# A gated mix of a state-space layer and a long convolution: mirrored lower halves, products over all frequencies at once, additions by accumulating transfers, loads spread by chunks

## The chip, the cores and the metric

The kernel runs on one core of one Trainium2 chip. The metric is the device time of one execution in microseconds. Three runs of the kernel before gave 442.48, 444.34 and 444.47 us; the median is 444.34. The engines are named as in the profile: PE is TensorE (PEld its weight loads), DVE VectorE, ACT ScalarE, POOL GpSimd, SP SyncE.

## The reference

Inputs are bf16, with S = 2048 rows and D = 1024 columns. The result is `g * a + (1 - g) * b`.

```python
x = A_x
g = sigmoid((x * gate_w).sum(-1, keepdims=True))
# a: a diagonal complex state space of P = 1024 states
Lam_bar = exp(dt * Lam); B_bar = ((Lam_bar - 1) / Lam)[:, None] * Bmat
Bu = einsum("bld,pd->blp", x, B_bar)
for t in range(L): h = Lam_bar * h + Bu[:, t]
a = 2 * einsum("blp,dp->bld", hseq, Cmat).real + x * Dskip
# b: a 4-tap shift of k, times v, then a causal convolution over all 2048 rows
kv = shift(k, shift_k) * v
y = irfft(rfft(kv, 2 * S) * rfft(ssm_k, 2 * S))[:S].astype(bf16)
b = x * (y + kv * ssm_D)
```

## The kernel before

The work has two stages. The first is the convolution, over eight chunks of 128 of the 1024 columns. The second is the state space, over four blocks of 512 rows (`tb`), each with four groups `g` of 256 states.

A chunk of the convolution goes like this. Time is cut in four blocks of 512. `taps` multiplies the transposed k (`kT`, columns on the partitions) by diagonal matrices `dg` of the four taps, and `times_v` multiplies the result by the transposed v, the lower half of each block read backwards. The transform of a block of 512 is made with tables of 256 rows, so the block is folded first: `fold_K` forms upper half plus and minus mirrored lower half of the convolution kernel with the matrices `ident` and `refl`, `fold_V` does the same for v times k with `PM`. Both are matmuls whose results ScalarE brings from PSUM to `eok` and `eov`. `fwd_K` and `fwd_V` then make the spectra `Kh` and `Vh` of 512 frequencies in four tiles (`psk`, `psv`, 128 frequencies each). `products` multiplies the spectra of the four blocks as complex numbers, each kernel block with each earlier or equal block of v, and sums them in `G`; it works on two halves of two frequency tiles each, in bf16 on VectorE (operations `t<-Kh,Vh` and `G<-G,t`). `inverse` goes back to time (`psz`), ScalarE moves the result to `cv`, and SP writes it to the scratch tensor `cv_scr` in DRAM.

The state space: `Bu` multiplies x by B (`bu`), ScalarE moves the result to `U`; `scan` turns it by the tables `TCi`, `TSi`, runs the recurrence as four scans (`W`), turns back by `TC`, `TS` and leaves `hb`; `Cy` multiplies by C (`psy`). `turn_table` makes the four tables of 128 states on ScalarE and VectorE, one per convolution chunk. The rest (`scale_b`, `scale_a`, `finish`) mixes the row tiles with the gate and writes them out; two of its additions are accumulating transfers issued by POOL (`gather`), and `loads` reads `cv_scr` and x again.

Every instruction of an engine is put in the order in which the program states it, by the helper `put` (line 97 of the profile, so nearly all groups carry that line). The order is written out by hand: generators such as `products`, `inverse` or `turn_table` are advanced a step at a time (`step`, `run`) in the loop over chunks (lines 764 to 819), so chunk c's products, chunk c-1's inverse, chunk c+1's spectra and chunk c+2's taps run side by side. In one turn of that loop TensorE's order is foldk, psz (half), psk (half), foldv, psz (half), psv (half), taps, psk (half), psv (half). After the loop (lines 829 to 861) the last chunk's products and inverse run beside the first `Bu`. SP issues all transposing loads, plain loads and stores in program order: per chunk `kT`, `kn`, `vT`, one table of B (`load_BT`, two transposes) or of x (`load_xT`), and the `cv_scr` stores; the C tables (`load_CT`) come in parts from line 832 on.

Memory is given out by pools with a number of buffers: 3 for loads (`ld`), 6 for spectra (`kvh`), 4 for `G`, three pairs of PSUM banks and two single banks.

Of the kernel before, what the change touches and what calls it, by code (L numbers as in the profile page):

```python
# [20 lines left out]
def kernel(  # L21
# [38 lines left out]
    TB = 512  # L60
# [3 lines left out]
    NFI = 4  # L64

# [5 lines left out]
    cv_scr = dram.tile([S, D], BF16, name="cv_scr")  # L71
# [3 lines left out]
    wk = pool("wk", 3)  # L75
# [4 lines left out]
    def w4(shape, dt, name):  # L80
        return wk.tile(shape, dt, name=name, tag="w4")
# [6 lines left out]

    def ps1(tag):
        return psum1.tile([128, 512], F32, name=tag, tag=tag)  # L90
# [49 lines left out]
    kv_pool = h3pool(h3, "kvh", 6)  # L140
    g_pool = h3pool(h3, "gh", 4)
    cv_pool = h3pool(h3, "cv", 2)
    tab_pool = h3pool(h3, "tab", 1)
    ld = h3pool(h3r, "ld", 3, side="right")
    ks_pool = h3pool(h3r, "ks", 2, side="right")
    eo_pool = h3pool(h3r, "eo", 2, side="right")
# [5 lines left out]
    prow = rows_[64:96, 0:128]  # L152

    nc.scalar.dma_start(out=skr, in_=B_shift_k.rearrange("(j p) k -> j p k", p=128))
    for i, ap in enumerate((A_Lambda_re, A_Lambda_im, A_log_dt, gate_w)):
        nc.scalar.dma_start(out=prow[i * 8:(i + 1) * 8, :], in_=ap.rearrange("(j p) -> j p", p=128))
# [4 lines left out]
    def load(which, c):  # L161
        cc = slice(c * 128, (c + 1) * 128)
        if which == "kn":

            t = ld.tile([128, NT, 128], BF16, name="kn", tag="ld")
            load_t(t, B_ssm_k[cc, :])
        else:
            t = ld.tile([128, S], BF16, name=which, tag="ld")
            load_t(t, (kf if which == "kT" else vf)[:, cc])
        lds[which, c] = t  # L170

    load("kT", 0)
    load("vT", 0)
# [5 lines left out]
    def load_BT(g):  # L179
        for c, src in enumerate((A_B_re, A_B_im)):  # L180
            load_t(BT[g][:, c], src[g * 256:(g + 1) * 256, :])

    def load_xT(tb, home=None):
        xT = (home or xt_pool).tile([128, ND, TB], BF16, name="xT")
        load_t(xT, xf[tb * TB:(tb + 1) * TB, :])
        xTs[tb] = xT
# [35 lines left out]

    zeros = w4([128, 512], BF16, "zeros")
    put("dve", V.memset, zeros, 0.0)
    pih = consts.tile([128, 1], F32, name="pih")
    put("dve", V.memset, pih, math.pi / 2.0)
# [8 lines left out]
    colm_i = iota_i32([128, 2], [[256, 2]], 1, 2, "colm")  # L235
    fr_i = iota_i32([128, 2, 256], [[2, 2], [4, 256]], 1, 0, "fr_")
# [6 lines left out]
    pcol = consts.tile([128, 4 + KS, ND], F32, name="pcol")  # L243
    gwb = consts.tile([128, ND], BF16, name="gwb")
    psp = ps1("p1")[:, 0:32 + ND * KS]
    raise_clock(3)
    for k in range(KS):
        mm(psp[:, 32 + ND * k:32 + ND * (k + 1)], skr[:, :, k], ident[32:32 + ND, 32:32 + ND], True, True)
    raise_clock(6)
    copy(pcol[:, 4:], psp[:, 32:].rearrange("p (i j) -> p i j", j=ND))  # L250

    def dgs(c, on_dve=False):
        dg = ks_pool.tile([128, KS, 128], BF16, name="dg", bufs=1)
        for k in range(KS):
            if on_dve:
                ts(dg[:, k], ident, pcol[:, 4 + k, c:c + 1], None, ALU.mult)
            else:
                act(dg[:, k], ident, func=ACT.Identity, scale=pcol[:, 4 + k, c:c + 1])
        return dg

    dg0 = dgs(0, True)
    colm = consts.tile([128, 2], F32, name="colm")
    ts(colm, colm_i, 1.0 / 4096.0, None, ALU.mult)
    fr_ = u4([128, 512], F32, "fr_")
    copy(fr_, flat(fr_i))
    hf = u4([128, 2, 512], F32, "h")
    for mt in range(2):
        ts(hf[:, mt], fr_, colm[:, mt:mt + 1], None, ALU.mult)
    rqf = reduced(flat(hf), 1024)
    put("dve", V.scalar_tensor_tensor, out=flat(hf), in0=rqf, scalar=-1.0, in1=rqf, op0=ALU.mult, op1=ALU.max)  # L270
    PM = consts.tile([128, 2, 2, 128], BF16, name="PM")
    for a in range(2):
        for b in range(2):
            ts(PM[:, a, b], ident, -1.0 if a and b else 1.0, None, ALU.mult)

# [9 lines left out]
    def inverse_angles(h2):  # L285
        hi = (w4 if h2 else u4)([128, 2, 512], F32, "h")
# [3 lines left out]
        rq = (u4 if h2 else w4)([128, 1024], F32, "rq")  # L290
        ts(rq, flat(hi), MAGIC, -MAGIC, ALU.add, ALU.add)
        tt(flat(hi), flat(hi), rq, ALU.subtract)
        return flat(hi)

    def inverse_table(h2, rq):
        sincos(rq, 1024, flat(SI[:, 2 * h2:2 * h2 + 2]), flat(CI[:, 2 * h2:2 * h2 + 2]), -TWO_PI)


    Lre, Lim, logdt = pcol[:, 0], pcol[:, 1], pcol[:, 2]
# [4 lines left out]
    TC = rot_pool.tile([128, NP, TB], BF16, name="TC")  # L304
    TS = rot_pool.tile([128, NP, TB], BF16, name="TS")
    TCi = rot_pool.tile([128, NP, TB], BF16, name="TCi")
    TSi = rot_pool.tile([128, NP, TB], BF16, name="TSi")
# [3 lines left out]

    def state_params():

        mm(psp[:, 0:32], prow, ident[64:96, 64:96], True, True)
# [85 lines left out]
    def rev(ap):  # L400

        return ap.rearrange("p (b t) -> p b t", t=512)[:, :, 255::-1]
# [560 lines left out]
```

## Time and profile before

| What | Value |
|---|---|
| median of three runs | 444.34 us |
| the profiled execution | 444.19 us |
| its span, first to last instruction | 442.4 us |
| granted TensorE clock, mean | 0.994 |
| products of chunk 0, 1, 2, 3 begin at | 21.7, 50.2, 74.6, 99.6 us |
| products of chunk 4, 5, 6, 7 begin at | 124.6, 149.6, 174.6, 199.5 us |
| first operation of the first scan begins at | 226.2 us |
| last scan's last operation ends, about | 425.5 us |
| last matmul ends, about | 436.8 us |

The profiled execution took 1.8 us more than its span. The page's first part gives each engine's busy time and its share of the span. The groups give, for operations of one line, engine and shape, how often they ran, their busy time, the mean length of one in ns, and how long the engine stood idle before them and for what. The chain of waits follows the work back from the last instruction: each piece is what the next one waited for. A matmul's length is longer than the distance to the next one, because matmuls are pipelined; distances are read from the chain or from the order of time.

### The profile page before, as it was taken

How to read it: one execution, taken by the hardware profiler on the slowest of the kernel's cores; microseconds unless marked ns; L12 is line 12 of the kernel's file. 1: busy time of each engine (PE TensorE's matmuls, PEld its weight loads, DVE VectorE, ACT ScalarE, POOL GpSimd, SP SyncE). 2: the span in 40 equal slices, each digit the busy share in tenths (PEclk: the TensorE clock that was granted, in tenths of full speed). 3: DMA queues.
4: the chain of work that ended last, by engine and by line, in shares of the span. 5: the costliest groups of instructions: out<-in, count | busy, mean ns of one | idle time of the engine just before them, and what ended most of it. 6: DMA issues, size and time to landing. Idle time of an engine off the chain costs nothing.

```text
span 442.4 us, 5684 instructions
## 1 busy us (share of the span) xinstructions
PE 423.1 (96%) x2104; PEld 199.4 (45%) x2142; DVE 421.9 (95%) x662; ACT 260.3 (59%) x320; POOL 27.1 (6%) x41
## 2 busy tenths in 40 slices
PE   8888899999999999979999999999999999999994
PEld 3434354544545454534444544444444444444442
DVE  7897999999999999999999999999999999999973
ACT  3796978979797979695552423443324432567102
POOL 2000000000000000000000000011011100223100
PEclk9998999999999999999999999999999999999999
DMA  7685294756558291135608941144474546297512
GB/s 144 144 134 105 49 184 100 140 111 149 125 102 184 60 205 24 25 68 100 115 12 159 176 135 24 25 119 111 99 172 96 147 139 166 38 207 162 118 45 98
DMA packets 128062, 49.94 MB, mean 113 GB/s; under 512 B 118169, under 2 KB 118177, under 8 KB 128034
## 3 DMA queue, kind: packets, MB, share of 16 engines
q1 hardware_dynamic: 123920, 42.22, 43.3%
q0 software_dynamic: 4032, 7.34, 9.6%
q8 instruction: 16, 0.26, 0.2%
q14 instruction: 12, 0.10, 0.1%
q10 hardware_dynamic: 82, 0.02, 0.0%
HBM read 8.67 MB, written 8.39 MB: 39 GB/s over the span
## 4 chain that ended last, share of the span: by engine, by line
PE 75%; DVE 12%; ACT 8%; issue 4%; DVEq 0%
PE bu L97 25%; PE psy L97 22%; PE psz L97 9%; PE psk L97 8%; DVE G L97 5%; DVE t L97 4%; PE taps L97 2%; PE foldk L97 2%; PE psv L97 2%; ACT Vh L97 2%; PE p L97 2%; PE foldv L97 2%; ACT eok L97 1%; ACT eov L97 1%; ACT Kh L97 1%
## 5 line engine op out<-in xcount | busy, mean ns | idle before, releaser
L97 PE MATMUL bu<-xT,BT 128*128 128x512 bf16 x499 | 111.6, 379 | 0.6
L97 DVE TENSOR_TENSOR t<-Kh,Vh 128x2048 bf16<-128x2048 bf16 (+3 forms) x128 | 102.3, 820 | 4.1 <-ACT SI L97 2.7
L97 PE MATMUL psy<-CT,hb 128*128 128x512 bf16 x470 | 105.2, 379 | 0.6
L97 PEld LDWEIGHTS <-BT 128*128 128x128 bf16 x512 | 50.0, 98 | 60.2
L97 PEld LDWEIGHTS <-hb 128*128 128x128 bf16 x512 | 49.9, 98 | 59.9
L97 DVE TENSOR_TENSOR G<-G,t 128x1536 bf16<-128x1536 bf16 (+2 forms) x144 | 69.4, 510 | 0.5
L97 ACT ACTIVATE U<-bu 128x1024 bf16<-128x1024 f32 x32 | 32.6, 1022 | 47.1 <-PE bu L97 42.3
L97 DVE TENSOR_TENSOR_SCAN W<-rv,init,A 128x512 bf16<-128x512 f32 x48 | 57.8, 1266 | 0.0
L97 PE MATMUL psz<-G,CI 128*128 128x512 bf16 x128 | 48.6, 379 | 2.0 <-DVE G L97 2.0
L97 PE MATMUL psz<-G,SI 128*128 128x512 bf16 x128 | 48.5, 379 | 0.0
L97 ACT ACTIVATE Kh<-psk 128x1024 bf16<-128x1024 f32 x32 | 32.6, 1028 | 10.7 <-PE psk L97 10.0
L97 ACT ACTIVATE ga<-psy,gcols 128x1024 bf16<-128x1024 f32 x8 | 8.9, 1114 | 46.3 <-PE psy L97 46.3
L97 PE MATMUL taps<-kT,dg 128*128 128x512 bf16 (+3 forms) x128 | 30.8, 385 | 1.6 <-ACT Vh L97 1.5
L97 ACT ACTIVATE Vh<-psv 128x1024 bf16<-128x1024 f32 x32 | 30.9, 1024 | 0.9 <-PE psv L97 0.9
L97 POOL DMA_DIRECT2D pbb<-gd x12 | 10.5, 871 | 342.4 <-ACT gd L97 330.3
L97 PE MATMUL psk<-eok,CF 128*128 128x512 bf16 (+1 forms) x96 | 26.5, 366 | 3.9 <-ACT eok L97 2.1
L97 ACT ACTIVATE cv<-psz 128x1024 bf16<-128x1024 f32 x16 | 16.4, 1027 | 23.0 <-PE psz L97 23.0
L97 PEld LDWEIGHTS <-CF 128*128 128x128 bf16 x160 | 15.7, 98 | 22.2 <-issue 7.0
L97 PE MATMUL psk<-eok,SF 128*128 128x512 bf16 (+1 forms) x89 | 24.7, 373 | 0.4
L97 ACT ACTIVATE BT<-psy,gcols 128x1024 bf16<-128x1024 f32 x6 | 6.7, 1111 | 30.6 <-PE psy L97 30.6
L97 PEld LDWEIGHTS <-SF 128*128 128x128 bf16 x160 | 15.9, 99 | 18.2 <-issue 3.5
L97 PE MATMUL psv<-eov,CF 128*128 128x512 bf16 x64 | 19.3, 379 | 3.0 <-ACT eov L97 2.2
(139 smaller groups left out, 570.0 us busy)
## 6 DMA issues: line engine op xcount, KB each, us to landing
cv_scr<-cv SPq DMA_DIRECT2D x32, 128.0 KB, 2.1
pbb<-cv_scr SPq DMA_DIRECT2D x12, 256.0 KB, 2.7
xr<-in_A_x_dram SPq DMA_DIRECT2D x12, 256.0 KB, 4.2
pbb<-gd POOLq DMA_DIRECT2D x12, 256.0 KB, 3.3
ga<-xr POOLq DMA_DIRECT2D x8, 256.0 KB, 3.3
out_dram<-ga SPq DMA_DIRECT2D x8, 256.0 KB, 2.0
out_dram<-BT SPq DMA_DIRECT2D x8, 256.0 KB, 2.0
BT<-cv_scr SPq DMA_DIRECT2D x4, 256.0 KB, 3.3
```

Of the source, the lines that this page charges most:

```text
L97: i = f(*a, **kw)
```

## The change

It touches nearly all of the first stage, and the joint to the second.

- v is loaded untransposed by plain copies (`v`, rows on the partitions), from chunk 2 on in pairs of chunks. `tap_sums` therefore makes its result with rows on the partitions: `kT` is the stationary operand, 128 rows at a time, and `dg` the moving one, 64 matmuls of 128 columns for a chunk. `kT` has 16 zero columns ahead, set by POOL.
- The folding matmuls are replaced. `mirror_K` and `mirror` only mirror the lower half with `refl` (into `lo`, by ScalarE); the difference is made by VectorE (`eok[:, 0]`, `ev`), the sum by an accumulating transfer (`eok[:, 1]`, `ks`). Chunks 0 to 2 keep `fold_K`; chunks 1 and 7 make the sum of v by VectorE, chunk 0 works from PSUM.
- From chunk 1 on `products` runs once over all 512 frequencies. It keeps the second factor's products in `T2` (memory of `BT[2]`) and subtracts and adds them at the end; the products with the next kernel block are added into `G` by an accumulating transfer of 128 x 3072, which VectorE does itself in the second half of chunk 0 and in chunk 7. The spectra `Kh` of even chunks lie in `BT[3]`.
- TensorE's order in a turn is psz (half), mirror, psz (half), psk of all four tiles, mirror_K, taps, psv of all four tiles.
- `turn_table` rounds with one operation on VectorE instead of two; its last two additions become one accumulating transfer into `TCSi`. The state's small factors (`c2r`, `c2i`, `mc2i`) are made with fewer, wider VectorE operations.
- In the start, `dg` of chunk 0 is made by ScalarE, `PM` is gone, `kT` of chunk 0 comes in two halves; one half of the inverse tables is made before the loop, one in chunk 0.
- Loads: B tables 0 and 1 in chunks 2 and 4, x blocks 0 and 1 in halves in chunks 5 and 6, B tables 2 and 3 in the last chunk, all C tables after the convolution's memory is given back.
- In the last chunk `Bu(0, 0)` stands ahead of the inverse of chunk 6 on TensorE.
- `cv_scr` is laid out by chunk, so its stores are long pieces and its loads short ones. PSUM has four pairs of banks and no single ones. Work memory of the scans lies where the convolution's was.
- At the end each row tile's last eight matmuls are followed by its own finishing work, and the last tile is written in two halves.

```diff
-    psum = pool("psum", 3, space=bass.MemoryType.PSUM)
-    psum1 = pool("psum1", 1, space=bass.MemoryType.PSUM)
+    psum = pool("psum", 4, space=bass.MemoryType.PSUM)
...
-    kv_pool = h3pool(h3, "kvh", 6)
-    g_pool = h3pool(h3, "gh", 4)
+    kv_pool = h3pool(h3, "kvh", 3)
+    g_pool = h3pool(h3, "gh", 2)
...
+            w = 1 if c < 2 else 2
...
+            move(t.rearrange("p n k d -> p n (k d)"),
+                 vf.rearrange("(n p) d -> p n d", p=128)[:, :, c * 128:(c + w) * 128])
...
+        act(rq, trow[0], func=ACT.Identity, scale=thn[:, pi:pi + 1], bias=magic)
         yield
-        ts(rq, h, MAGIC, -MAGIC, ALU.add, ALU.add)
-        tt(rq, h, rq, ALU.subtract)
+        put("dve", nc.vector.scalar_tensor_tensor, out=rq, in0=rq, scalar=-MAGIC, in1=h, op0=ALU.add, op1=ALU.subtract)
...
-        act(TCi[:, pi], TC[:, pi], func=ACT.Identity, scale=c2r[:, pi:pi + 1])
-        act(TSi[:, pi], TS[:, pi], func=ACT.Identity, scale=c2r[:, pi:pi + 1])
-        yield
-        tt(TCi[:, pi], TCi[:, pi], m[:, 0], ALU.add)
-        tt(TSi[:, pi], TSi[:, pi], m[:, 1], ALU.add)
+        act(flat(TCSi[:, pi]), flat(TCS[:, pi]), func=ACT.Identity, scale=c2r[:, pi:pi + 1])
+        gather(flat(TCSi[:, pi]), flat(m))
...
+    def mirror_K(c):
+        kb = lds.pop(("kn", c)).rearrange("p (a f) d -> p f a d", f=4)
+        ps = ps2([128, 2, 4, 128], "mirror")
+        for mt in range(2):
+            mm(ps[:, mt], refl[:, 1], kb[:, 1 - mt], True, mt == 0)
+            if mt == 1:
+                mm(ps[:, mt, 0], refl[0:1, 1], sD[:, c * 128:(c + 1) * 128], False, True)
+        eo = eos["k", c] = eo_pool.tile([128, 2, 2, 4, 128], BF16, name="eok")
+        lo = eo_pool.tile([128, 2, 4, 128], BF16, name="lo", bufs=2)
+        act(lo, ps, func=ACT.Copy)
+        act(eo[:, 1], kb[:, 2:4], func=ACT.Copy)
+        yield
+        tt(eo[:, 0], kb[:, 2:4], lo, ALU.subtract)
+        gather(eo[:, 1], lo)
...
+    def tap_sums(kT, dg, h):
+        ps = ps2([128, 8, 128], "taps")
+        for n in range(8):
+            t0 = (8 * h + n) * 128
+            for i in range(KS):
+                k0 = PAD + t0 - i
+                mm(ps[:, n], kT[:, k0:k0 + 128], dg[:, i], i == 0, i == KS - 1)
+        return ps
...
+    def mirror(c):
+        ps = ps2([128, 2, 4, 128], "mirror")
+        for mt in range(2):
+            mm(ps[:, mt], refl[:, 1], kss[c][:, 1 - mt], True, True)
+        return ps
...
+    def times_v(c):
+        ks, v = kss[c], lds.pop(("v", c))
+        tt(ks, ks, v.rearrange("p (b q) d -> p q b d", q=4), ALU.mult)
+        yield
+        lo = eo_pool.tile([128, 2, 4, 128], BF16, name="lo", bufs=2)
+        act(lo, mirror(c), func=ACT.Copy)
+        yield
+        e = eo_pool.tile([128, 2, 4, 128], BF16, name="ev")
+        tt(e, ks[:, 2:4], lo, ALU.subtract)
+        if c in (1, NC - 1):
+            tt(ks[:, 2:4], ks[:, 2:4], lo, ALU.add)
+        else:
+            gather(ks[:, 2:4], lo)
...
+    def products(c, h=0, home=u4, by_dma=True):
...
+        mult(0, 0, None, G)
+        yield
+        n1 = mult(1, 0, W1)
+        if by_dma:
+            gather(G[:, :, 1:], n1)
+        yield
+        t2 = mult(0, 1, T2)
+        yield
+        n2 = mult(1, 1, W2)
+        if not by_dma:
+            tt(G[:, :, 1:], G[:, :, 1:], n1, ALU.add)
+        n3 = mult(2, 1, home([128, 4 * w], BF16, "t"))
+        tt(t2[:, :, 1:], t2[:, :, 1:], n2, ALU.add)
+        n2 = mult(3, 1, home([128, 2 * w], BF16, "t"))
+        tt(t2[:, :, 2:], t2[:, :, 2:], n3, ALU.add)
+        n1 = mult(2, 0, W2[:, 0:4 * w])
+        n3 = mult(3, 0, W2[:, 4 * w:])
+        tt(t2[:, :, 3:], t2[:, :, 3:], n2, ALU.add)
+        tt(n1[:, :, 1:], n1[:, :, 1:], n3, ALU.add)
+        yield
+        tt(G[:, :, 2:], G[:, :, 2:], n1, ALU.add)
+        yield
+        tt(G[:, 0], G[:, 0], t2[:, 1], ALU.subtract)
+        tt(G[:, 1], G[:, 1], t2[:, 0], ALU.add)
...
+        tabs, back, prod = turn_table(c - 1, u4), inverse(c - 1), products(c)
+        step(old)
+        step(tabs)
+        step(back)
+        step(tv)
+        steps(prod, 3)
+        run(tv)
+        step(old)
+        if nn < NC:
+            dg = dgs(nn)
+        run(back)
+        run(old)
+        if c in (1, 3):
+            load("v", c + 3)
+        elif c == NC - 2:
+            load_xT(1)
+        fwd_K(n)
+        step(prod)
+        fk = none
+        if nn < NC:
+            fk = mirror_K(nn)
+            step(fk)
+            taps(nn, dg)
+        step(tabs)
+        step(prod)
+        run(fk)
+        run(prod)
+        if nn < NC:
+            tv = times_v(nn)
+            step(tv)
+        fwd_V(n)
+        old = tabs
...
+        prod, back = products(c, 0, room, False), inverse(c - 1)
+        load_BT(2, 0)
+        load_BT(2, 1)
+        load_BT(3, 0)
+        load_BT(3, 1)
...
+        Bu(0, 0)
+        steps(prod, 3)
...
-    for pi in range(4, NP):
+    for pi in range(NP):
         load_CT(pi)
+    move(drow, bc(A_Dskip.rearrange("(o d) -> o d", o=1), [128, D]))
...
     for tl in range(4):
-        Cy_g(tb, tl, pss[tl][0], NG - 1, False, [0])
-    for tl in range(4):
-        Cy_g(tb, tl, pss[tl][0], NG - 1, True, [1])
-        if tl % 2 == 0:
+        Cy_g(tb, tl, pss[tl][0], NG - 1, True)
+        if tl == 1:
             scale_a(t0 + tl, pss[tl][1])
-    for tl in (1, 0, 3, 2):
         run(fins[tl])
```

More of the change, by code (lines that the diff above doesn't have):

```diff
@@ L678, in scale_b, with Cy_g @@
         gather(pbb, gd)
[L680 removed]
+    def Cy_g(tb, tl, ps, g, last):
         tsl = slice(tl * 128, (tl + 1) * 128)
[L682 removed]
+        for j in range(2):
             for c in range(2):
```

593 lines of the change are left out of this document (279 added, 314 removed).

## The prediction

> **What bounds the kernel now.** I read the page's first two parts, then the busy time stage by stage with the borders at the chunks, then the chain of waits, then the groups by shape, last the transfers. The page names no single bound: two engines are nearly full.
>
> ```profile
> span 442.4 us, 5684 instructions
> PE 423.1 (96%) x2104; PEld 199.4 (45%) x2142; DVE 421.9 (95%) x662; ACT 260.3 (59%) x320; POOL 27.1 (6%) x41
> ```
>
> The stages separate them. A stage's columns are its length, then busy time of TensorE, its weight loads, VectorE, ScalarE, GpSimd, then clock and DMA share.
>
> ```profile
> 99.60:124.60 25.00, 24.68 (x126) 12.14 (x127) 24.90 (x46) 21.66 (x29) 0.00 (x0) 1.00 0.63 138
> ...
> 199.50:226.20 26.70, 26.54 (x121) 12.09 (x124) 26.26 (x49) 16.30 (x23) 0.00 (x0) 1.00 0.45 87
> 226.20:425.50 199.30, 198.30 (x1019) 92.17 (x1037) 197.39 (x237) 78.30 (x82) 23.41 (x27) 1.00 0.51 117
> 425.50:436.80 11.30, 11.25 (x52) 4.88 (x51) 4.59 (x7) 1.89 (x2) 0.86 (x1) 1.00 0.20 47
> ```
>
> A convolution chunk takes 25.0 us (products start at 74.6, 99.6, 124.6, 149.6, 174.6): VectorE 24.9, TensorE 24.7, ScalarE 21.7. From 199.5 to 436.8 TensorE has no gap: 237.3 us in which only TensorE counts. The chain of waits (start, length, work) shows the handover, the end, and the pace of a row of matmuls:
>
> ```profile
> 62.40 1.75 PE foldv L97 x16
> ...
> 199.13 0.30 DVE G L97
> 199.44 0.04 issue
> 199.48 2.75 PE psz L97 x12
> ...
> 209.14 3.45 PE psz L97 x16
> ...
> 428.48 6.71 issue
> 435.19 0.25 DVE BT L97
> ```
>
> TensorE waited 1.99 us at 199.48 for the products of chunk 6. So: what is saved before 199.5 moves the dense stretch forward whole; what is saved on VectorE inside it is worth nothing (VectorE idles 6.71 us at the end). Prices come from the groups (mean ns of one):
>
> ```profile
> L97 DVE TENSOR_TENSOR t<-Kh,Vh 128x2048 bf16<-128x2048 bf16 x32 | 37.7, 1219 | 1.2 <-ACT Kh L97 1.2
> L97 DVE TENSOR_TENSOR t<-Kh,Vh 128x512 bf16<-128x512 bf16 x32 | 13.5, 421 | 0.0
> L97 ACT ACTIVATE Kh<-psk 128x1024 bf16<-128x1024 f32 x32 | 32.6, 1028 | 10.7 <-PE psk L97 10.0
> L97 POOL DMA_DIRECT2D pbb<-gd x12 | 10.5, 871 | 342.4 <-ACT gd L97 330.3
> ```
>
> Last the transfers, by queue (packets, MB, share of 16 engines) and by issue (KB each, us to landing):
>
> ```profile
> q1 hardware_dynamic: 123920, 42.22, 43.3%
> q0 software_dynamic: 4032, 7.34, 9.6%
> pbb<-gd POOLq DMA_DIRECT2D x12, 256.0 KB, 3.3
> BT<-xr POOLq DMA_DIRECT2D x4, 256.0 KB, 4.7
> ```
>
> **Parts and costs.** *VectorE in a chunk.* 2048 against 512 elements give 798 ns per 1536: 0.52 ns each and 155 ns fixed. Three neighbours (2048, 2048, 1536) take 3.22 us, not 3.39, so each follows 0.085 us before the last one ends: 0.07 us fixed. Before, a chunk has 39,936 elements in 42 such operations and two f32 ones of 512 (0.95 us): 20.75 + 2.94 + 0.95 = 24.6; measured 25.0, a factor 1.016. After, both halves are one: mults of 4096, 3072, 4096, 3072, 2048, 1024, 2048, 1024, adds of 3072, 2048, 1024, 1024, 2048, 2048, 2048, then ev 1024, eok 1024 and the product with v, 2048: 37,888 elements, 18 operations, one f32 of 512 (0.61). 19.7 + 1.26 + 0.61 = 21.55, times 1.016 = **21.9**. The additions that left (3072 into G, 1024 each for ks and eok, 1024 for TCi/TSi) became accumulating transfers.
>
> *TensorE in a chunk.* 512 columns cost 0.2155 us (16 psz in 3.45). psz 6.9, psk 6.05, psv 3.46 stay. foldk (10, 2.15 us) becomes mirror_K (3, 0.55), foldv (16, 1.75) becomes mirror (2, 0.43). taps keep 8192 columns, but as 64 weight-load and matmul pairs of 128 columns instead of 16 of 512. No row shows such a pair: below is 24.7 ns (64 gate pairs of 1 column, 1.58 us on the chain), above 109 ns (16 foldv pairs of 256 columns, 1.75 us). From 512 columns at 215.5 and 256 at 109.4 a straight line gives 56; I take it, for both neighbours lie on it: 64 x 56 = 3.6. Sum 17.4 + 3.6 = **21.0**; ends 19.0 and 24.4.
>
> The Trainium skill (TensorE: Matmul & The Clock Gate, Back-to-back issue gap) gives about 81 ns for such a pair in a sustained stream. By it taps would cost 5.2 and TensorE 22.6, 0.7 over VectorE. For 512 columns it gives 131 ns, where this trace has 215, so I hold it for the less likely price.
>
> *ScalarE in a chunk.* Evictions follow one another at 0.92: 14 (cv 2, lo 2, Kh 4, ks 2, Vh 4) = 12.9; eok from SBUF 1.04; dg 1.15; hr twice, abs, two sines, m twice 4.2; TCSi as one of 1024 1.04: 20.3 (16 evictions, 20.7 before). It stays under the others by 1 us, which is its whole cover; if it is short, Vh comes late and VectorE's next first product waits.
>
> *The coupling.* Before, products began on the first half of the frequencies while the second was still made. Now the first product waits for all four Vh, the last work of TensorE and ScalarE in the chunk, and VectorE's whole queue stands behind it. psz of the previous chunk can start when G is ready, 1.1 us before that product; 21.0 of TensorE and 1.0 of the last eviction then end at 20.9 of the 21.9: cover 1.0. I take no stall; bounds 0 and 2 us a chunk (ScalarE's longest wait for psk in the row above, 10.7 over 32 evictions, is a third of a microsecond each).
>
> *Accumulating transfers, POOL.* Per chunk four issues (0.87 us each before; POOL had nothing there) move 768 + 3 x 256 KB. 7.34 MB in 9.6% of 442.4 us is 173 GB/s: 9.1 us of all engines. By the hardware queue (42.22 MB in 43.3%: 220 GB/s) kT, kn, a share of v and cv, 1.84 MB, take 8.3, in chunks 2 and 4 with BT 10.7. 17 to 20 of 21.9 us, against 0.63 of 25. G's is consumed 12 us after its issue, by an addition of VectorE with eok, the last G and the product with v behind it; eok's and TCSi's in the next chunk. Tight is ks: it is issued about 8 us after the chunk's first product begins (behind ev, which reads ks), on the queue behind G's, issued at 4 (two products); psv reads it at about 16.5. At the queue's rate it lands at 4 + 1 (issue) + 4.5 (G) + 1.5 + 1.8 (3.3 us to landing less 1.5 of moving) = 13; at half rate 19. I take 13 to 16, for the other queue's share here was 0.63 and falls: no wait.
>
> *Start.* Half loads of kT and a copy of v instead of a transpose let taps begin earlier; dg (0.74) moves to ScalarE, PM (0.49) and five small operations go, but four operations read PSUM in f32 with 1024 elements (512 cost 681 ns, so 1.13 in sequence, 4.5 for 2.7 before). VectorE begins at 2, has 18.2 of its own and about 0.9 of waits: first product at 21.1 (21.7 before). To the first product of chunk 1: two halves 35,328 elements, 31 operations 20.5; ks 2.3; ev, ks, dg, small ones 3.0; waits 0.6: 26.4 against 28.5. ScalarE, which held this stretch before with both inverse tables (6 us), now has four of their six operations there: 19 evictions 17.5, tables 4, small 0.8 = 22.3, under 26.4. Chunk 1 starts at **47.5**, before 50.2; ends 45 and 50.
>
> *Last chunk.* TensorE now runs Bu(0,0) (6.9) ahead of psz of chunk 6, so the 1.99 us wait goes. Next late is psz of chunk 7, at 27.6 in the dense stretch; its products end at about 26: cover 1.6. BT 2 and 3, loaded only there, are four transposes of about 2.7: in by 14, used at 20.7 and 34.5. CT comes whole after the tables are free: SP starts xT(2) at 36 (35.9 before), 5.1, then 16 CT at 1.34 and 4 to land: 67; first used at 70. Cover 3 us; if gone, that stalls TensorE one to one. drow, pbb and xr queue behind on SP to 64, used by ScalarE after 70. The scan's A and hb now lie on memory of the last Kh, Vh and G, which VectorE and TensorE have left by then: nothing. cv written in long pieces and read in short ones lies beside the scan stage, read a step ahead. The fourth PSUM pair removes waits like the 0.51 us of psv for Kh at 195.56: below 1 us a chunk, put at nothing. The tail: both last row halves go through VectorE after the last matmul, 0.2 + 1.4 and the 3.4 from VectorE's end to the span's end: 5.0, before 5.6.
>
> *Sum.* Chunk 1 at 47.5; four chunks 87.6; G of chunk 5 20.7; then TensorE psz, mirror, psk, psv 17.0; dense stretch 237.3; tail 5.0: span 415.1. The profiled execution took 444.19, 1.8 over its span (median shown 444.34): **417**.
>
> **Rivals.** (1) taps pairs above the line, or ScalarE's handshake, set the chunk. For: idle cover is 1 us. At 109 ns, period 24.4: 4 x 2.5, about 1 in chunk 5 and 3 in the start: 431. Midway, 82 ns, period 22.7: 4 x 0.8 + 1 = 421.
> (2) ks lands late and psv, hence Vh and the next first product, waits; five chunks have this order. If transfers queued with transposes land each 256 KB at 4.7 us (the slowest row): 4 + 4 x 4.7 = 22.7, 6.2 late, 5 x 6.2 = 31: 448, slower. Decides from 5.4 us late ((444.2 - 417) / 5). Against: 4.7 contains the fixed part once per transfer; share was 0.63. At 2 us late: 427.
> The Trainium skill (DMA: Bandwidth & Descriptors, Issuing engines are not separate DMA queues) speaks for this rival: whichever engine issues, the same 16 engines do the work, interleaved.
> (3) The late CT or BT stall TensorE 3 to 8 us: 420 to 425.
> No rival is that VectorE sets the scan stage: it starts the scans at 173 + 26 = 199 and needs 199.3, ending at 398, while TensorE ends at 410.
>
> **How the numbers follow.** Forecast 0.57 (412 to 422); rival 1 0.20 (418 to 431); rival 2 0.15, of which 0.08 slower and 0.03 without change; rival 3 0.06; something unseen 0.02, slower. Range 410 to 432: the low end from a start of 45 (2.5), no 1.016 (1.7) and 0.5 us of PSUM waits gone in each of six chunks; the high end is rival 1's. Over 0.5% (2.2 us, about what a measurement here can tell) faster: 0.57 + 0.20 + 0.04 + 0.06 = 0.87; within 0.03; slower 0.10.
>
> **What would show it.** Products of chunks 2 to 5 starting every 22 us with VectorE full; chunk 1 at 47.5; Bu(0,0) from about 173; no TensorE gap for 237 us. taps' 64 matmuls in 3.6 us. Wrong: psv waiting for a DMA into ks, the first product waiting for Vh over 1 us, psy waiting for CT.

## The result and the profile after

The changed kernel takes 415.38 us in the median, the kernel before, run beside it, 443.55: a ratio of 0.936, with a 95% interval of 0.933 to 0.940. Forecast were 417.0 us in a range of 410 to 432. Some executions ran longer at a lower granted clock, one of the changed kernel's four (426.43 us) and three of four of the kernel below that puts the inverse of chunk 6 first, and the ratios leave them out. The profiled execution took 415.12 us, its span is 413.3.

The page's first part and the busy time by stages, of the changed kernel. The columns of a stage are its borders and length, busy time of TensorE, weight loads, VectorE, ScalarE and GpSimd (instructions in brackets), granted clock, DMA share, GB/s.

```profile
span 413.3 us, 6053 instructions
PE 402.1 (97%) x2340; PEld 201.5 (49%) x2378; DVE 399.5 (97%) x470; ACT 253.3 (61%) x307; POOL 53.0 (13%) x74
```

```profile
69.00:90.60 21.60, 21.20 (x149) 11.77 (x149) 21.60 (x21) 20.00 (x27) 3.89 (x5) 1.00 1.19 190
170.90:197.70 26.80, 26.64 (x123) 12.18 (x125) 26.70 (x24) 22.52 (x31) 2.57 (x3) 1.00 0.69 141
197.70:397.00 199.30, 198.24 (x1018) 92.14 (x1037) 197.76 (x237) 78.27 (x82) 23.22 (x27) 1.00 0.61 128
397.00:409.10 12.10, 12.05 (x56) 5.26 (x54) 5.79 (x8) 1.11 (x1) 0.86 (x1) 1.00 0.30 87
```

A chunk lasts 21.6 us where it lasted 25.0, and VectorE is busy for all of it, in 21 instructions instead of 46. The scan stage has the length it had (199.3 us) and starts 28.5 us earlier. The two engines' shares of the span hardly moved, 96% to 97% and 95% to 97%; they say nothing of what was gained.

The groups by shape (instructions, busy us, mean ns, idle time before them) and the transfers (by queue: packets, MB, share of 16 engines; by issue: KB each, median us to landing), of the changed kernel:

```profile
L91 PE MATMUL psz<-G,SI 128*128 128x512 bf16 x128 | 48.5, 379 | 1.9 <-DVE G L91 1.9
L91 PE MATMUL taps<-dg,kT 128*128 128x128 bf16 x512 | 31.1, 223 | 0.0
L91 DVE TENSOR_TENSOR G<-Kh,Vh 128x4096 bf16<-128x4096 bf16 x4 | 9.1, 2282 | 0.0
L91 POOL DMA_DIRECT2D G<-wkh x7 | 8.5, 1221 | 70.5 <-DVE wkh L91 70.5
```

```profile
q1 hardware_dynamic: 117648, 42.22, 47.3%
q0 software_dynamic: 8528, 17.17, 25.4%
G<-wkh POOLq DMA_DIRECT2D x6, 768.0 KB, 7.1
ks<-lo POOLq DMA_DIRECT2D x5, 256.0 KB, 6.9
```

All idle time of TensorE in the chunks that VectorE causes is 1.9 us in five waits for G. The software queue moves 17.17 MB instead of 7.34. The instructions of one chunk in order of time (start, length), VectorE first, then ScalarE, then GpSimd, where a bracket would give idle time ahead:

```profile
87.16 2.35 DVE L91 TENSOR_TENSOR G<-G,BT 128x2048 bf16<-128x2048 bf16 x2
89.43 1.22 DVE L91 TENSOR_TENSOR ks<-ks,v 128x2048 bf16<-128x2048 bf16 x1
90.57 2.28 DVE L91 TENSOR_TENSOR G<-Kh,Vh 128x4096 bf16<-128x4096 bf16 x1
...
86.55 3.77 ACT L91 ACTIVATE Vh<-psv 128x1024 bf16<-128x1024 f32 x4
...
73.24 1.20 POOL L91 DMA_DIRECT2D G<-wkh  x1 [7.35 <-DVE wkh L91]
76.05 0.89 POOL L91 DMA_DIRECT2D ks<-lo  x1 [1.61 <-DVE ev L91]
```

The coupling is in the first four rows: the last Vh ends at 86.55 + 3.77 = 90.32, the first product of the next chunk starts at 90.57 without a wait. It is held up by VectorE's own queue, but only 0.25 us separate it from waiting for ScalarE. The transfer into ks is issued at 76.05 and lands 7.6 us later, at 83.7 (6.9 is the median of the five); psv takes it at 85.9.

Where the 29.1 us of span went (starts of products and of the dense stretch, end of the last matmul):

| Stretch | before | after | gained |
|---|---|---|---|
| start to the products of chunk 1 | 50.2 | 47.4 | 2.8 |
| four chunks | 99.4 | 86.3 | 13.1 |
| products of chunk 5 to the dense stretch | 49.9 | 37.2 | 12.7 |
| dense stretch to the last matmul | 237.3 | 238.2 | -0.9 |
| tail | 5.6 | 4.2 | 1.4 |

Two rows of this table need a second look. What the first row gains is idle time of VectorE: between the first product of chunk 0 and that of chunk 1 it was busy for 25.45 of 28.5 us before and for 26.06 of 26.8 after. Before, 2.65 us of that idle time were a wait for ScalarE's inverse table `SI`. Part of the gain may belong to the clock: in the profile before, the granted clock of this stretch was 0.94, in the profile after 1.00.

```profile
21.70:50.20 28.50, 23.40 (x108) 10.92 (x108) 25.45 (x57) 23.35 (x33) 0.00 (x0) 0.94 0.59 105
```

The kernel before also has spans of 440.7 us at a mean clock of 0.997 to 0.998, beside the profiled 442.4 at 0.994, so up to 1.7 of the 2.8 us may not come from the change. The dense stretch, the other row, did not become slower by 0.9 us; it holds more work. The kernel before ran four matmuls of the inverse of chunk 6 ahead of its wait at 199.48.

```profile
196.47 0.38 PE L97 MATMUL psz<-G,CI 128*128 128x512 bf16 x1
...
197.12 0.38 PE L97 MATMUL psz<-G,SI 128*128 128x512 bf16 x1
```

In the changed kernel these stand behind Bu(0,0), inside the stretch: four times 0.2155 us are 0.86.

### The profile page after: what moved, and what is told of

Same layout as the page of the kernel before. It is cut to its first block, busy times and chain, and to the rows that moved or that the text cites. A ratio compares the mean times of both kernels' runs of the same rounds, so it can differ in the third digit from the quotient of the medians.

```text
span 413.3 us, 6053 instructions
## 1 busy us (share of the span) xinstructions
PE 402.1 (97%) x2340; PEld 201.5 (49%) x2378; DVE 399.5 (97%) x470; ACT 253.3 (61%) x307; POOL 53.0 (13%) x74
## 3 DMA queue, kind: packets, MB, share of 16 engines
q1 hardware_dynamic: 117648, 42.22, 47.3%
q0 software_dynamic: 8528, 17.17, 25.4%
## 5 line engine op out<-in xcount | busy, mean ns | idle before, releaser
L91 PE MATMUL psy<-CT,hb 128*128 128x512 bf16 x502 | 111.4, 379 | 0.6
L91 ACT ACTIVATE U<-bu 128x1024 bf16<-128x1024 f32 x32 | 32.4, 1021 | 48.1 <-PE bu L91 43.3
L91 PE MATMUL psz<-G,SI 128*128 128x512 bf16 x128 | 48.5, 379 | 1.9 <-DVE G L91 1.9
L91 PE MATMUL psz<-G,CI 128*128 128x512 bf16 x128 | 48.5, 379 | 0.1
L91 PE MATMUL taps<-dg,kT 128*128 128x128 bf16 x512 | 31.1, 223 | 0.0
L91 PEld LDWEIGHTS <-kT 128*128 128x128 bf16 x512 | 29.8, 100 | 0.7
L91 ACT ACTIVATE BT<-psy,gcols 128x1024 bf16<-128x1024 f32 x5 | 5.6, 1113 | 30.4 <-PE psy L91 30.4
L91 PE MATMUL psk<-eok,CF 128*128 128x512 bf16 (+1 forms) x89 | 24.0, 360 | 0.0
L91 DVE TENSOR_TENSOR wkh<-BT,Vh 128x3072 bf16<-128x3072 bf16 (+4 forms) x20 | 21.8, 1109 | 0.0
L91 PEld LDWEIGHTS <-CI 128*128 128x128 bf16 x128 | 12.5, 98 | 18.2 <-issue 3.3
L91 DVE TENSOR_TENSOR wkh<-Kh,Vh 128x3072 bf16<-128x3072 bf16 (+2 forms) x16 | 21.3, 1348 | 0.0
L91 DVE TENSOR_TENSOR hb<-TCS,W 128x2048 bf16<-128x2048 bf16 (+1 forms) x17 | 19.8, 1163 | 1.2
```

The costliest lines, as they stand in the source:

```text
L91: i = f(*a, **kw)
```

## The experiments

The theory: a chunk is as long as the sum of VectorE's own instructions, the loop through TensorE and ScalarE (G of one chunk to the first product of the chunk after the next) lies just under it, and what is saved ahead of the dense stretch moves the end one for one. Rivals: TensorE (21.2 of 21.6 us busy) is the bound already; the transfers pace the chunk.

### VectorE makes the sum into G again

```diff
+        by_dma = False
         if by_dma:
             gather(G[:, :, 1:], n1)
```

> One part undone: the sum of 128 x 3072 into G is made by VectorE in every chunk, where the changed kernel leaves it to an accumulating transfer in all but the second half of chunk 0 and chunk 7. Theory A (a chunk is as long as VectorE's own instructions, 21.6 us of 21.6): such an addition took 1.75 us alone and 1.66 in a row, so the chunk becomes 23.2 to 23.3; chunks 1 to 5 and half an addition in chunk 0 make 5 x 1.66 + 0.85 = +9.2, about 424.6 us. Rival B (transfers or TensorE, with 21.2 of 21.6 busy, pace the chunk as much as VectorE does): taking 768 KB off the queues gives some of it back, and the time rises by 5 us or less.

Measured: 425.33 us, span 423.0, 9.7 more than the changed kernel's. Two stages of one chunk each, and the landing of ks's transfer:

```profile
71.20:94.45 23.25, 22.57 (x151) 12.21 (x151) 23.25 (x21) 18.29 (x25) 2.67 (x4) 0.96 0.59 118
94.45:117.70 23.25, 21.35 (x149) 11.67 (x149) 23.25 (x22) 21.94 (x30) 2.67 (x4) 0.99 0.74 150
```

```profile
ks<-lo POOLq DMA_DIRECT2D x5, 256.0 KB, 3.7
```

The period is 23.25: 1.67 more, the price of the operation, and VectorE is still busy for all of it. Theory A holds; the transfers give nothing back though their share of the chunk falls from about 1 to 0.6 or 0.7. ks lands in 3.7 us instead of 6.9: half of its way is G's transfer ahead of it.

### Two halves again

```diff
-        k = 2 if c == 0 else 1
+        k = 2 if c < NC - 1 else 1
...
+    def both(c):
+        hs = [products(c, h) for h in range(2)]
+        for _ in range(6):
+            for p in hs:
+                step(p)
+            yield
...
-        tabs, back, prod = turn_table(c - 1, u4), inverse(c - 1), products(c)
+        tabs, back, prod = turn_table(c - 1, u4), inverse(c - 1), both(c)
```

> One part undone: products of chunks 1 to 6 are made in two halves of the frequencies again, in turns (each operation on the first half, then on the second). The elements stay; a chunk gets 15 more operations of VectorE at 0.07 us fixed: +1.05, and one issue more on GpSimd (about 1 us). Theory A: period 22.6, over 5 chunks +5.3, about 420.7 us. Rival B (the earlier start of the first product, which needs only two of the four Vh, gives some back, or TensorE gets G earlier): VectorE is full, so nothing is to be had from it, unless its operations then wait less than 0.1 us a chunk; under +3.

Measured: 420.49 us, span 418.8 (+5.5). One chunk:

```profile
70.35:92.94 22.59, 21.49 (x149) 11.71 (x149) 22.59 (x35) 20.96 (x28) 5.15 (x6) 1.00 1.00 184
```

The period is 22.59, 1.02 longer for 15 operations more: 0.068 us of fixed cost for each, where the prediction had read 0.07 from three neighbours. The earlier first product gave nothing back. So the width of the operations is worth 5 us of the 28, the accumulating sum into G nearly 10. These two, and the order in the last chunk further down, are the parts of the change that were undone alone; the smaller sums by transfer, the mirroring matmuls and the start were not.

### TensorE: the mirror of v made twice and four times

```diff
-        for mt in range(2):
+        for mt in range(2) if c < 2 else (0, 1) * 2:
             mm(ps[:, mt], refl[:, 1], kss[c][:, 1 - mt], True, True)
```

(`* 4` in the second kernel.)

> TensorE gets 0.43 us more in each turn from chunk 1 on: the two mirroring matmuls of v are made twice, the second time over the first, with the same result. Theory A with the coupling (the first product waits for the last Vh, which came 0.25 us before it): 0.43 less 0.25 is 0.2 us a chunk for chunks 1 to 5, and 0.43 whole in the turn of chunk 6, where nothing on VectorE stands behind: +1.3, about 416.7; period 21.8. Rival B (TensorE's own free time, 0.5 to 0.7 us a chunk, takes it): period 21.6, only the last turn pays, +0.4. Rival C (TensorE is the bound already): 6 x 0.43 = +2.6.

> The same with three repeats, 1.29 us more of TensorE in a turn. With the coupling's 0.25 us of cover: 5 x 1.04 + 1.29 = +6.5, about 421.9, period 22.6, and the first product now waits for Vh. With a cover of 1.0 us, as predicted: 5 x 0.29 + 1.29 = +2.7, about 418.1, period 21.9. TensorE the bound already: 6 x 1.29 = +7.7.

Measured: ratios to the kernel before of 0.940 (0.938 to 0.943; span 414.4, +1.1) and 0.949 (0.947 to 0.951; 420.71 us, span 418.8, +5.5). VectorE's first products and one stage of the four-fold mirror:

```profile
92.52 2.29 DVE L91 TENSOR_TENSOR G<-Kh,Vh 128x4096 bf16<-128x4096 bf16 x1 [0.75 <-ACT Vh L91]
114.92 2.29 DVE L91 TENSOR_TENSOR G<-BT,Vh 128x4096 bf16<-128x4096 bf16 x1 [0.75 <-ACT Vh L91]
137.34 2.29 DVE L91 TENSOR_TENSOR G<-Kh,Vh 128x4096 bf16<-128x4096 bf16 x1 [0.75 <-ACT Vh L91]
```

```profile
92.50:114.90 22.40, 22.30 (x155) 12.38 (x155) 21.66 (x19) 20.76 (x28) 3.92 (x5) 1.00 0.85 169
```

Now TensorE is full (22.30 of 22.40) and VectorE waits 0.75 us a chunk for Vh, as rival 1 would have it. The period rose by 0.83 for 1.29 added: the cover is 0.46 us, between the 0.25 that one chunk of the trace shows and the predicted 1.0. The sum 5 x 0.83 + 1.29 = 5.4 comes close to the 5.5 measured, but in part by luck: in the rows, the products of chunk 6 start 111.7 us after those of chunk 1 where it was 107.9 (+3.85, for the first of the five periods is 22.1), 0.6 us come from a later start whose code is the same, and 1.0 comes after them. The smaller repeat agrees with such a cover: there it is 108.3 us (+0.09 a chunk for 0.43 added), 0.25 us come from the start, and the last turn pays 0.4. TensorE was not the bound, but it is half a microsecond from it: by this cover, the taps at the 82 ns of the midway case of rival 1 (1.7 us more) would have cost some 1.2 us a chunk, an estimate.

### ScalarE: one eviction more, early or late in the chunk

```diff
             act(cv, ps, func=ACT.Copy)
+            if l2 == 0 and c < NC - 2:
+                act(cv, ps, func=ACT.Copy)
```

```diff
             act(of_tile(VH[c], fi), ps, func=ACT.Copy, scale=2.0 / 1024.0)
+            if fi == 0 and c > 1:
+                act(of_tile(VH[c], fi), ps, func=ACT.Copy, scale=2.0 / 1024.0)
```

> ScalarE gets one eviction more per turn, early in the chunk: the first half of cv is brought from PSUM twice (0.92 us in sequence) for chunks 0 to 5. ScalarE's sum rises from 20.0-20.5 to 20.9-21.4 of 21.6. In the changed kernel ScalarE waited behind this place three to four times in a chunk (0.34 and 0.49 us for psk, 0.47 for taps): theory A, the wait for psk and taps takes the extra work, the last Vh comes as before and the period stays 21.6: 0 to +1 us. Rival B (ScalarE's cover is only the 0.25 us by which the last Vh came before the first product, wherever the work is put): 0.92 less 0.25 makes 0.67 a chunk, +3.4 us.

> The same 0.92 us of ScalarE, but in its last row of the chunk: the first of the four Vh is brought twice, from chunk 2 on. Theory A: four evictions stand in one row from the last ks to the first product, with nothing to take it up but the cover of the coupling; the four-fold mirror left 0.46 us of it unseen (1.29 added, period 21.57 to 22.40). So 0.92 less 0.25 to 0.46 is 0.5 to 0.7 a chunk for chunks 1 to 5, and in the last turn psv of chunk 7 may wait for a PSUM pair: +2.5 to +4.3, 418 to 420 us, period 22.1 to 22.2. If a chunk's cover were the predicted 1.0 us: 0 to +0.5.

Measured: early a ratio of 0.9365 (0.934 to 0.939) and a span of 413.2, that is nothing; late a ratio of 0.953 (0.947 to 0.958), from single executions of 418.5, 420.2 and 423.6 us (a fourth took 424.8), the first of them profiled with a span of 416.7 (+3.4). A stage with the early eviction, and VectorE's first products of chunks 2 to 5 with the late one:

```profile
90.50:112.00 21.50, 21.09 (x149) 11.76 (x149) 21.50 (x20) 21.16 (x29) 3.92 (x5) 1.00 0.83 158
```

```profile
69.16 2.29 DVE L91 TENSOR_TENSOR G<-BT,Vh 128x4096 bf16<-128x4096 bf16 x1 [0.18 <-ACT Vh L91]
91.31 2.29 DVE L91 TENSOR_TENSOR G<-Kh,Vh 128x4096 bf16<-128x4096 bf16 x1 [0.49 <-ACT Vh L91]
113.16 2.29 DVE L91 TENSOR_TENSOR G<-BT,Vh 128x4096 bf16<-128x4096 bf16 x1 [0.18 <-ACT Vh L91]
137.09 2.29 DVE L91 TENSOR_TENSOR G<-Kh,Vh 128x4096 bf16<-128x4096 bf16 x1 [2.27 <-ACT Vh L91]
```

ScalarE at 21.16 of 21.5 us costs nothing as long as the work lies ahead of the waits for psk and taps that take it up; behind them the same 0.92 us makes VectorE wait 0.2 to 0.5 a chunk. That is less than the expected 0.5 to 0.7, so that the +3.4 lies in the expected range by luck: most of it is the 2.27, and that is something else. In that chunk TensorE stood before psv, and the transfer into ks took up to 11.3 us to land:

```profile
131.60 0.59 PE L91 MATMUL psv<-ks,SF 128*128 128x512 bf16 x2 [1.89 <-DMA ks<-lo]
```

The issue was at 120.22, so psv wanted ks 131.60 - 1.89 - 120.22 = 9.5 us after the issue. In the changed kernel's profile psv takes ks 9.2 to 9.8 us after the issue and the landings took 6.6 to 8.8, which leaves covers of 1.0 to 3.2 us in the five chunks; a landing of 11.3 breaks them. The next chunk had such a wait too (1.07 us), and the two-halves kernel had two, the longest 1.3 us. Rival 2's place is real; in the changed kernel's profile it stays just unseen. Whether it also makes the difference between the executions is open, since only one was profiled.

### The transfers delayed

```diff
             gather(G[:, :, 1:], n1)
+            if 0 < c < NC - 1:
+                gather(G[:, :, 1:], n1)
```

> In chunks 1 to 6 the accumulating transfer into G is made twice, so the output counts the products with the next kernel block twice. GpSimd must let the first one land (7 us) before it issues the second, and the issue of ks's transfer stands behind that: about 6 us later than now, and 768 KB more are under way beside it. Rival 2 of the prediction (ks late, psv and the next chunk's first product wait): ks landed at about 83 for a use at 85.4 in the chunk that starts at 69.0, so it comes 3 to 7 us late, and 5 chunks with 0.25 us of further cover make +14 to +32, 430 to 447; the trace shows TensorE's psv waiting for the transfer into ks. If the transfers have room and psv can wait unseen: under +3.

Measured: 449.85 us, 1.7% slower than the kernel before (ratio 1.017, 1.013 to 1.020); the profiled execution is the fastest of the four, with a span of 443.9, +30.6. Waits of TensorE, of VectorE and of GpSimd, in order of time:

```profile
74.72 1.01 PE L91 MATMUL psv<-ks,SF 128*128 128x512 bf16 x2 [10.36 <-DMA ks<-lo]
100.08 0.59 PE L91 MATMUL psv<-ks,SF 128*128 128x512 bf16 x2 [2.74 <-DMA ks<-lo]
...
73.25 1.22 DVE L91 TENSOR_TENSOR G<-G,wkh 128x2048 bf16<-128x2048 bf16 x1 [8.63 <-DMA G<-wkh]
98.30 1.23 DVE L91 TENSOR_TENSOR G<-G,wkh 128x2048 bf16<-128x2048 bf16 x1 [1.17 <-DMA G<-wkh]
...
91.62 1.19 POOL L91 DMA_DIRECT2D G<-wkh  x1 [5.56 <-DMA G<-wkh]
92.36 1.38 POOL L91 DMA_DIRECT2D ks<-lo  x1
```

GpSimd holds ks's issue until the first transfer into G has landed (5.56 us at 91.62). The issue of ks comes 4.7 to 5.5 us later in the chunk than in the changed kernel. Over five chunks psv waited 26.2 us for ks, and VectorE's addition of G waited as well; Vh and the next chunk's products come late behind both. The two longest waits, 10.4 and 6.9 us, are those in which the landing was longer too (14.4 and 11.7 us after the issue, 7.3 to 7.7 in the other three), and in these two chunks the granted clock was 0.84 and 0.89. VectorE's work, TensorE's and ScalarE's are those of the changed kernel: the whole gain is lost by one transfer more in that queue. The prediction put the point from which this decides at 5.4 us late in each of five chunks; 26.2 / 5 = 5.2 us late, together with the waits for G, ended above it.

### ks's transfer ahead of G's

Can the thin cover be widened? VectorE makes T2 first and the product with the next kernel block third, so the small transfer goes first.

```diff
-        n1 = mult(1, 0, W1)
-        if by_dma:
-            gather(G[:, :, 1:], n1)
-        yield
         t2 = mult(0, 1, T2)
         yield
+        n1 = mult(1, 0, W1)
+        if by_dma:
+            gather(G[:, :, 1:], n1)
+        yield
...
-        steps(prod, 3)
+        steps(prod, 2)
         run(tv)
+        step(prod)
```

> The changed kernel with one reordering in chunks 1 to 6: VectorE makes T2 before the product with the next kernel block, so that ks's transfer is issued ahead of G's instead of behind it. VectorE's operations are the same. Theory A (VectorE's sum): period 21.6 and the time of the changed kernel, 415 +/- 1. Of the transfers: ks, which landed 6.6 to 8.8 us after its issue (11.3 in the run with four Vh and one more), lands in 3.3 to 4.5 us as it did without G's transfer ahead (3.7), so its cover before psv grows from 2 to about 7 us; G's keeps its 7 us and is issued 1.3 us later, with 2 to 3 us left before the addition that reads G. Rival: G's transfer is now late, that addition waits 1 us or more a chunk, +5.

Measured: 419.16 us, a ratio of 0.945 (0.942 to 0.948); the profiled span is 416.1 (+2.8). The landings, and VectorE's two waits:

```profile
G<-wkh POOLq DMA_DIRECT2D x6, 768.0 KB, 8.9
ks<-lo POOLq DMA_DIRECT2D x5, 256.0 KB, 3.4
```

```profile
65.94 1.23 DVE L91 TENSOR_TENSOR G<-G,wkh 128x2048 bf16<-128x2048 bf16 x1 [2.00 <-DMA G<-wkh]
...
131.29 1.23 DVE L91 TENSOR_TENSOR G<-G,wkh 128x2048 bf16<-128x2048 bf16 x1 [0.37 <-DMA G<-wkh]
```

The rival is right: ks lands in 3.4 us as expected, but G's transfer did not keep its 7 us, it takes 8.9, and it starts later. In chunk 1 the addition that reads G waits 2.0 us, in chunk 4 0.37; the other periods are 21.6 to 21.7. The Trainium skill (DMA: Bandwidth & Descriptors, Issuing engines are not separate DMA queues) says that transfers end up on the same 16 engines and interleave, whichever engine issued them. These two runs show the sharing (what ks gains, 3.5 us, G loses in part, 1.8), but both transfers are issued by GpSimd. The order of the changed kernel, in which neither transfer is late, is the better one.

### One operation of VectorE's given to GpSimd

On that order, two more edits: the difference `eok[:, 0]` by GpSimd, and the first product in two halves of the frequencies, so that it needs two of the four Vh only. The second kernel also makes the sum of the second half of chunk 0 by transfer.

```diff
-        tt(eo[:, 0], kb[:, 2:4], lo, ALU.subtract)
+        put("pool", nc.gpsimd.tensor_tensor, out=eo[:, 0], in0=kb[:, 2:4], in1=lo, op=ALU.subtract)
...
-        mult(0, 0, None, G)
+        if 0 < c < NC - 1:
+            for q in (slice(0, w // 2), slice(w // 2, w)):
+                tt(G[:, :, :, q], bc(K[:, 0:1, :, q], [128, 2, 4, w // 2]), Vt[:, :, :, q], ALU.mult)
+        else:
+            mult(0, 0, None, G)
...
-            p1 = products(0, 1, by_dma=False)
+            p1 = products(0, 1)
```

> The order of the run before, and two more edits in chunks 1 to 6: the difference eok[:, 0] (0.60 us of VectorE in a row) is made by GpSimd, which is 13% busy, and the first product is split in two halves of the frequencies, so that its first half (0.07 us more in all) needs two of the four Vh only. VectorE's sum falls from 21.57 to 21.04. Theory A: TensorE's 21.13 to 21.2 is then the bound, the period falls by 0.3 to 0.4, 5 chunks: -1.5 to -2.2, about 413.3 us. Rival (VectorE and GpSimd disturb one another, or GpSimd's subtraction is so long that eok or the transfer behind it is late): the period stays or grows, 415 or more.

> The run before, and in chunk 0 the second half's sum into G by transfer too, where VectorE (full from 2 us on) had made it with one operation of 128 x 1536, 0.87 us in a row. Theory A: the products of chunk 1 start 0.8 us earlier and all that follows with them: -0.8 on the run before, about 412.5. Rival (ScalarE, with 22.3 of these 26.3 us, or the transfer's 4 to 7 us, takes its place): 0 to +1.

Measured: 423.72 us (span 423.0) and 423.32 us (span 421.9). Groups by shape and three rows in order of time, of the first of the two:

```profile
L91 POOL TENSOR_TENSOR eok<-kn,lo 128x1024 bf16<-128x1024 bf16 x5 | 23.6, 4713 | 23.5 <-ACT lo L91 23.5
L91 DVE TENSOR_TENSOR G<-G,BT 128x2048 bf16<-128x2048 bf16 x12 | 17.8, 1521 | 0.2
```

```profile
110.25 5.29 POOL L91 TENSOR_TENSOR eok<-kn,lo 128x1024 bf16<-128x1024 bf16 x1 [4.50 <-ACT lo L91]
...
113.59 4.16 DVE L91 TENSOR_TENSOR G<-G,BT 128x2048 bf16<-128x2048 bf16 x2
...
136.73 1.73 DVE L91 TENSOR_TENSOR G<-G,wkh 128x2048 bf16<-128x2048 bf16 x1 [1.34 <-DMA G<-wkh]
```

The rival is right again. What costs VectorE 0.68 us alone takes GpSimd 4.7 from start to end, and VectorE's own additions stretch: the two of G took 4.16 us together instead of 2.35 (in two chunks of five; in two others the addition ahead of them is stretched), their mean over all chunks 1521 ns instead of 1216. The periods are 23.0 to 24.6. (The Trainium skill, SBUF — State Buffer, section SBUF: two separate sides, says that VectorE and GpSimd share one pair of ports, taken whole by one of them when an operation of VectorE has two inputs in SBUF and GpSimd reads it too. The stretched rows agree: beside GpSimd's subtraction, from 110.25 to 115.54, VectorE's operations keep their usual lengths until 113.56, and the addition that starts then is done only at about 116.6, 1.1 us after the subtraction.) G's transfer is late besides, by 4.1 us in three chunks. With the smaller edit of the second kernel the products of chunk 1 start at 46.5 instead of 48.1, or of the 47.4 that the same start took in the changed kernel, and the profiled span is 1.1 shorter; 0.8 were expected. The medians lie only 0.4 us apart and their intervals overlap, so that a gain in time is not shown. In the changed kernel it wasn't tried, and none of these versions beats the changed kernel.

### The order in the last chunk, undone and done alone

In the changed kernel the inverse of chunk 6 put ahead of Bu(0,0) again, and in the kernel before Bu(0,0) put ahead of it:

```diff
-        Bu(0, 0)
         steps(prod, 3)
         step(ta)
         step(tb_)
         run(ta)
         run(back)
+        Bu(0, 0)
         run(tb_)
```

```diff
     step(t)
+    Bu(0, 0)
     step(back)
     step(p0)
...
     step(t)
-    Bu(0, 0)
```

> One part undone: on TensorE the inverse of chunk 6 stands again ahead of Bu(0,0) in the last chunk. TensorE has done psv of chunk 7 at 170.9, and G of chunk 6 is ready at about 175.8 (its products start at 155.3, the last addition ends 20.5 later). Theory A: TensorE stands still for 4.9 us there, all later work moves by as much: +4.5 to +5, about 420 us. If the order on TensorE there is worth nothing (another wait ends later anyway): 0 to +1.

> The kernel before with one part of the change alone: Bu(0,0) stands ahead of the inverse of chunk 6 on TensorE. There TensorE waited 1.99 us for G of chunk 6 at 199.48. Theory A: that wait goes, and no more than that, since the chunks before it are as long as they were: -0.5 to -2.0, 442 to 444 us against 442.5 to 444.4 for the kernel before; in the changed kernel the same order was worth 5 us and more, because its shorter chunk leaves TensorE further ahead of VectorE. If the order is worth the same in both: -5.

Measured: 421.49 us and 443.2 us. The time of the first kernel is a single execution, and the profile is of another, with a span of 431.0 us, so that only the places and sizes of waits are read from it. TensorE's waits (total us, times, longest), of the first kernel and then of the second, there from 195 us on:

```profile
PE psz L91 <- DVE G L91: 6.0, 5, 4.2
```

```profile
PE psy L97 <- DVE hb L97: 0.6, 1, 0.6
PE bu L97 <- ACT U L97: 0.6, 1, 0.6
```

The wait for G of chunk 6 comes back, 4.2 us and 0.5 for its second part, and the time is 6 us longer, near the 5 expected. In the kernel before, the same order took away the 1.99 us wait, and two others came in its place, 0.56 for U from ScalarE and 0.6 for hb of the scan from VectorE: 0.6 us of span are left, and the ratio of 0.999 (0.997 to 1.001) does not tell it from nothing. The order is worth what VectorE lags behind TensorE at that point: it pays for the shorter chunk, it doesn't replace it.

## Why the prediction was right, point by point

| Step of the prediction | forecast | measured |
|---|---|---|
| VectorE in a chunk, the sum of its rows | 21.55 | 21.6, all of the period |
| factor 1.016 on it | 21.9 | not needed |
| taps, a pair of 128 columns | 56 ns, 3.6 us | 3.58 us for 64, 55.9 ns |
| TensorE, ScalarE in a chunk (2 to 5) | 21.0, 20.3 | 21.1 to 21.2, 20.0 to 20.5 |
| cover of the coupling | 1.0 | 0.25 in the trace, 0.46 by the four-fold mirror, 0.4 to 0.7 by the late eviction |
| ks lands after the chunk's first product | 13 to 16, used at 16.5 | 14 to 16, used at 16.3 to 16.9 |
| products of chunk 0 | 21.1 | 20.6 |
| products of chunk 1 | 47.5 | 47.4 |
| start of the dense stretch | 172.8 | 170.9 |
| dense stretch | 237.3 | 238.2 |
| tail | 5.0 | 4.2 |

**The main term** was right for its reason: the rows of the profile before, 0.52 ns an element and 0.07 us an operation, gave the new length of VectorE's queue to 0.05 us, and the two experiments that put operations back cost what that rule says (1.67 and 1.02 us a chunk). VectorE remained the bound by itself.

**The factor 1.016** was the mis-sized term that makes nearly all of the miss of 1.6 us. It was taken over from the chunk before, which was 25.0 us long for a sum of 24.6, and read as a loss that grows with the work. Without it five chunks end 1.7 us earlier, close to the 1.9 by which the dense stretch started ahead of the forecast. The tail, 0.8 us shorter, and the dense stretch, 0.9 longer, cancel: its length was taken over from the kernel before, without the four psz matmuls that the new order puts into it.

**The start** was right to 0.1 us by luck. Chunk 0 began 0.5 us earlier than forecast and took 0.4 us longer, and the same start took 47.3 to 48.5 us in the other kernels that leave it unchanged.

**The cover of the coupling** was mis-sized by half or more, and without effect on the time. It rested on a period of 21.9 and 21.0 us of TensorE; with 21.6 and 21.2 half of it is gone. The third of a microsecond that the prediction reads as ScalarE's longest wait for psk is a mean over 32 evictions; four waits ahead of 50.2 us make 4.6 of its 10.0 us, the longest 2.5. That it decides nothing in the changed kernel is shown by the first products, which start without a wait; that it is the next bound, by the four-fold mirror.

**The taps' price** by the straight line through the two neighbours with 256 and 512 columns was right, and the 81 ns of the Trainium skill (TensorE: Matmul & The Clock Gate, Back-to-back issue gap) are not what this trace shows for 64 pairs in a row: 55.9 ns each.

**Rival 2** did not happen in the profile, and the landing forecast for it was right, but its chance of 0.15 was not too much: its cover is 1.0 to 3.2 us, the landing reached 11.3 us in a kernel with hardly more work, and one transfer more turns the whole change into a loss. It happened in the profile of the kernel with the inverse of chunk 6 first, whose chunks 1 to 5 are those of the changed kernel: in chunk 4 psv waited 3.17 us for ks, in chunk 5 taps waited 3.75 us for the transfer of kT, and these chunks lasted 25.9 and 26.9 us. So the changed kernel's transfers can be late as they stand; how often is open. **Rival 3** had no sign: from 170.9 to 409.1 TensorE waited for nothing that the profile names; the last transposes of C were issued at 64.9 us of the dense stretch, forecast 67 for their landing, used at 70.7.

**The scan stage** is closer than the prediction put it. It said that VectorE would end well ahead of TensorE; so it did, the chain of waits of the changed kernel ends on TensorE,

```profile
403.33 5.79 PE psy L91 x26
409.12 0.02 issue
409.14 0.75 DVE BT L91
```

but between 238.9 and 296.8 us its pieces are VectorE's, the scans and the turning operations around them. TensorE has no wait there yet. More saved ahead of it on TensorE alone may meet VectorE there, as the reordered kernel before did; no run of the changed kernel shows it.

## What to carry to other kernels

Where an engine is busy for all of a repeated stage, its price list (ns an element, a fixed cost an operation) read from neighbouring rows forecasts the stage's new length without any factor, as long as each loop through the other engines is added up as well and is shorter; put a number on how much shorter, for that is the next bound. Work moved to accumulating transfers is free only while each landing stays ahead of its reader: add up issue, place in the queue and landing for every one of them, since an earlier transfer for one is a later one for another. Extra work on an engine that is not the bound costs nothing where a wait behind it takes it up; where none does, it costs what exceeds the cover, here 0.2 to 0.5 of 0.92 us.

## What the runs showed of the hardware that was not expected

GpSimd's subtraction of 128 x 1024 bf16 took 4.7 us on average (5.3 at most) against 0.68 on VectorE, part of it beside VectorE's operations, and stretched VectorE's additions from 2.35 to up to 4.16 us for two. A 256 KB accumulating transfer into ks landed in 3.4 to 3.7 us in the median where G's was not ahead of it on its queue (3.2 to 7.6 in all), and in 6.9 behind the 768 KB of G (6.6 to 8.8). With no more bytes in the chunk it once took 11.3. That one falls in chunk 4, as does the longest of the changed kernel, 8.8; a table of B is loaded there, but no run moved that load, and what lengthened the transfer stays open.
